# Delta-rule attention with a gated MLP on one core: one written list in place of a planner, and inverses widened two steps at a time

## The chip, the core and the metric

The kernel runs on one core of a Trainium2 chip. The metric is the device time of one execution in microseconds (us). The engines are named as the profile names them: PE (matmul; PEld is its weight load), DVE (VectorE), ACT (ScalarE), POOL (GpSimd) and SP, which issues the DMAs.

## What is computed

Thirty-two heads (batch 4, 8 heads, 48 columns each) run a delta rule over 768 positions; the result goes through an MLP whose gate mixes positions:

```
for t in range(S):
    y[:, :, t] = einsum('bhd,bhde->bhe', q[:, :, t], state)
    v_old = einsum('bhde,bhd->bhe', state, k_n[:, :, t])
    state = state + beta[:, :, t] * einsum('bhd,bhe->bhde', k_n[:, :, t], v[:, :, t] - v_old)
h = maximum(x @ w_in, 0)                 # x: y of all heads side by side, 4 x 768 x 384
u, v = h[..., :512], h[..., 512:]
v_s = einsum('ts,bsd->btd', w_spatial, layernorm(v)) + b_spatial
out = (u * v_s) @ w_out                  # 4 x 768 x 384
```

`k_n` is `k` divided by its norm. Weights `w_in` and `w_out` arrive as 64-bit floats and are decoded on the chip.

## The kernel before, in words

The 768 positions are cut into 12 chunks of 64. Inside a chunk the recurrence is solved by a 64x64 triangular inverse for each head, so that only the 48x48 state passes from one chunk to the next. Sixteen heads fill one pass over the tiles, so there are 24 *steps*: steps 0 to 11 are the 12 chunks of the first two batches, steps 12 to 23 those of the last two.

**Preparing.** The inverses are made for four steps at a time, in 6 *groups* (`prep`). For a group the PE forms the products of the keys (tile `ke` or `bn`, `kk`); ACT or DVE copy them from PSUM into a tile `xt`; a DVE transposition (L537) brings the 32x32 diagonal blocks into a layout, `la`, in which each of the 128 partitions holds whole blocks. A chain of small instructions (L545 to L555) works out the norms. Then the blocks are inverted column by column on all partitions at once, two DVE instructions a column (L574, L579; POOL does rows 16 to 31 beside it). Where `g < G16` (the first two groups) only 16x16 blocks are inverted this way (L587, L592), half the work, and a pair of PE blocks (`widen16`, 32 program matmuls each) makes 32x32 out of them. The DVE transposes back (L606). `widen` makes 64x64 out of 32x32: a DVE transposition into `tn` (L635), 16 matmuls of 32x32, a negation on ACT into `pi`, 16 more, and two copies.

**A step** (`step`): the PE forms k·state (`a`), DVE subtracts it from v (L738), the PE multiplies by the inverse (`b`), ACT evicts to `w` (L767), the PE forms the new part of the state (`c`), DVE adds it to `s` (L780), and only then can the next step's `a` run. `kqt` (L712 masks it) and `pu` make the output, which goes to `xs`. Each of these blocks is 16 program matmuls on two to four sub-tiles of the PE; an fp32 matmul leaves two records in the trace, so a block has 32.

**The MLP.** After every second step `mlp(J)` runs 128-row *dense* matmuls, 18 of 512 columns and 36 of 256; the gate of two batches (`mlp_g`, `mlp_o`) can start after step 11, that of the other two after step 23.

**Order.** All matmuls stand on line 486 (`mm`), all DMAs on line 381 (`ld`). `P.add` only records an instruction with a duration, a priority and its dependencies. `Plan.run` then lists them: it repeatedly takes, over all engines, the ready instruction that could start first by its own estimate, and among equals the one with the smaller priority, into which the table `TUNE` goes. An instruction with two possible engines (`both`: DVE or POOL) goes to the one that would end it sooner. Each engine executes its instructions in the order listed.

Of the kernel before, what the change touches and what calls it, by code (L numbers as in the profile page):

```python
# [25 lines left out]
NJ = NP // 2  # L26
KR = 112
EPS = 1e-6
G16 = 2
FILL = False  # L30

LOW, HIGH, KEEP, FORCE = 0.37, 0.74, 0.5, 0.4
WARM = 12.0
BIAS = 1.5

TUNE = [
# [10 lines left out]
]  # L47
GATE = 3.413
OTHER = {"DVE": "POOL", "POOL": "DVE"}
# [4 lines left out]

class Op:
    __slots__ = ("i", "eng", "dur", "fn", "pr", "deps", "out", "n", "acq", "rel", "give", "start", "end", "lag", "port", "kb", "took", "inst", "alt", "line", "bias", "act")


class Hold:
    def __init__(self):  # L60
        self.unit = None
        self.refs = 0
        self.t = 0.0
        self.tile = None
# [7 lines left out]
class Plan:  # L72


    LAT = {"PE": 0.2, "DVE": 0.06, "ACT": 0.08, "POOL": 0.08, "SP": 0.0, "X": 0.0}

    def __init__(self):
        self.ops, self.w, self.r, self.pools = [], {}, {}, {}
        self.filler, self.warm_from = None, 0.0
        self.kinds = {}  # L80

    def pool(self, name, units):
        self.pools[name] = [[0.0, u] for u in units]

    def add(self, eng, dur, fn, rd=(), wr=(), pr=0.0, acq=(), rel=(), give=(), lag=0.0, port=False, kb=0, inst=32, bias=0.0, act=1.0):
        o = Op()
        o.bias = bias
        o.kb, o.inst, o.act = kb, inst, act
        o.line = fn.__code__.co_firstlineno if fn is not None else 0
        o.alt = {}  # L90
        for e, d in dur.items() if isinstance(dur, dict) else ((eng, dur),):
            c = self.kinds.setdefault((e, o.line), len(self.kinds)) if fn is not None else -1
# [18 lines left out]
        for _, h in rel:  # L111
            h.refs += 1
# [962 lines left out]
```

## Time and profile before

| | |
|---|---|
| time, median of 3 runs | 526.24 us (526.05 to 527.23) |
| profiled execution | span 522.3 us |
| PE busy | 452.3 us, 87% of the span |
| DVE busy | 294.9 us, 56% |
| ACT busy | 246.8 us, 47% |
| POOL busy | 169.8 us, 32% |

The profiled execution is one execution; its span runs from the first to the last instruction, and the time of a run is 3.9 us more than this span. PE's granted clock changes between its two levels within the span; a block of small matmuls takes about 0.6 us at one and 1.0 us at the other.

### The profile page before, as it was taken

How to read it: one execution, taken by the hardware profiler on the slowest of the kernel's cores; microseconds unless marked ns; L12 is line 12 of the kernel's file. 1: busy time of each engine (PE TensorE's matmuls, PEld its weight loads, DVE VectorE, ACT ScalarE, POOL GpSimd, SP SyncE). 2: the span in 40 equal slices, each digit the busy share in tenths (PEclk: the TensorE clock that was granted, in tenths of full speed). 3: DMA queues.
4: the chain of work that ended last, by engine and by line, in shares of the span. 5: the costliest groups of instructions: out<-in, count | busy, mean ns of one | idle time of the engine just before them, and what ended most of it. 6: DMA issues, size and time to landing. Idle time of an engine off the chain costs nothing.

```text
span 522.3 us, 21286 instructions
## 1 busy us (share of the span) xinstructions
PE 452.3 (87%) x9544; PEld 410.4 (79%) x9544; DVE 294.9 (56%) x700; ACT 246.8 (47%) x530; POOL 169.8 (32%) x262
## 2 busy tenths in 40 slices
PE   4046789689889898877999899997999999999997
PEld 4045777679678787766989788886999899999997
DVE  3866675375775458876687777741353321453340
ACT  3947743653267735984235320842217874032111
POOL 2546765254416455465434642500000000000000
PEclk9999956655997879996899979996999999999999
DMA  8630254233241424104230422022000002001002
GB/s 291 236 124 26 90 198 131 64 107 110 75 128 35 156 102 141 52 2 151 75 120 33 152 90 95 31 75 82 11 1 0 2 1 75 16 1 62 31 0 92
DMA packets 16027, 42.63 MB, mean 82 GB/s; under 512 B 3392, under 2 KB 7616, under 8 KB 15936
## 3 DMA queue, kind: packets, MB, share of 16 engines
q1 hardware_dynamic: 15936, 41.27, 23.7%
q8 instruction: 75, 1.23, 1.0%
q14 instruction: 16, 0.13, 0.1%
HBM read 35.36 MB, written 4.72 MB: 77 GB/s over the span
## 4 chain that ended last, share of the span: by engine, by line
PE 77%; DVE 9%; issue 6%; ACT 3%; DMA 3%; SPq 1%; DVEq 0%; ACTq 0%
PE ps L486 77%; DMA vf<-in_w_in 2%; DVE prod L574 1%; SPq L381 1%; DVE ps L579 1%; DVE xt L606 1%; DVE ps L592 1%; DVE prod L587 1%; DMA ke<-in_k_t 1%; DVE pt L712 1%; ACT vr L866 0%; DVE nl L551 0%; ACT xs L797 0%; ACT ut L898 0%; ACT xt L513 0%
## 5 line engine op out<-in xcount | busy, mean ns | idle before, releaser
L486 PE MATMUL ps<-wsp_h,vf 128*128 128x256 f32 x480 | 99.4, 290 | 0.1
L486 PEld LDWEIGHTS ps<-wsp_h,vf 128*128 128x128 f32 x480 | 79.0, 191 | 2.0 <-issue 0.3
L486 PE MATMUL ps<-wsp_l,vf 128*128 128x256 f32 x240 | 68.1, 284 | 0.0
L486 PEld LDWEIGHTS ps<-wsp_l,vf 128*128 128x128 f32 x240 | 46.1, 192 | 0.1
L698 POOL TENSOR_TENSOR bn<-bn,nn 128x384 f32<-128x384 f32 x24 | 20.4, 852 | 74.6 <-DMA bn<-in_bun 36.9
L933 DVE TENSOR_TENSOR gt<-ps,bbc 128x512 f32<-128x512 f32 x24 | 16.6, 690 | 49.3 <-PE ps L486 49.1
L579 DVE TENSOR_TENSOR ps<-ps,prod 128x192 f32<-128x192 f32 (+13 forms) x120 | 39.5, 329 | 3.6
L574 DVE TENSOR_TENSOR prod<-ps,la 128x192 f32<-128x192 f32 (+13 forms) x120 | 38.4, 320 | 3.3
L486 PE MATMUL ps<-ke 48*64 48x64 f32 x704 | 19.1, 262 | 23.4 <-DVE pt L712 17.7
L486 PEld LDWEIGHTS ps<-ke 48*64 48x64 f32 x704 | 15.9, 168 | 27.5 <-DVE pt L712 17.9
L486 PE MATMUL ps<-bn 48*64 48x64 f32 x832 | 22.6, 259 | 7.4 <-DMA bn<-in_k_t 3.7
L767 ACT COPY w<-ps 128x384 f32<-128x384 f32 x24 | 11.5, 479 | 36.9 <-PE ps L486 36.9
L938 ACT CAST xt<-gt 128x512 fp32r<-128x512 f32 x12 | 7.5, 622 | 43.3 <-DVE gt L936 43.3
L780 DVE TENSOR_TENSOR s<-s,ps 112x384 f32<-112x384 f32 x20 | 11.0, 550 | 29.3 <-PE ps L486 29.3
L486 PE MATMUL ps<-tn,xt 32*32 32x32 f32 x768 | 21.2, 214 | 7.3 <-issue 3.3
L486 PE MATMUL ps<-wout_h,g 128*128 128x384 f32 x96 | 27.1, 355 | 0.0
L486 PEld LDWEIGHTS ps<-bn 48*64 48x64 f32 x832 | 19.1, 169 | 10.0 <-issue 7.5
L486 PEld LDWEIGHTS ps<-tn,xt 32*32 32x32 f32 x768 | 18.1, 128 | 10.2 <-DVE tn L635 3.9
L486 PE MATMUL ps<-wout_h,xt 128*128 128x384 f32 x96 | 25.5, 336 | 0.0
L656 ACT COPY xt<-ps 32x256 f32<-32x256 f32 x48 | 17.4, 362 | 16.2 <-PE ps L486 15.6
L797 ACT COPY xs<-ps 112x512 f32<-112x512 f32 x22 | 12.9, 586 | 23.3 <-PE ps L486 22.2
L486 PE MATMUL ps<-s,bn 48*64 48x48 f32 x704 | 19.0, 254 | 5.6 <-DVE s L780 4.7
(176 smaller groups left out, 1201.4 us busy)
## 6 DMA issues: line engine op xcount, KB each, us to landing
bn<-in_bun SPq DMA_DIRECT2D x22, 896.0 KB, 5.0
ke<-in_k_t SPq DMA_DIRECT2D x22, 256.0 KB, 3.0
out<-ob SPq DMA_DIRECT2D x24, 192.0 KB, 1.9
vf<-in_w_in SPq DMA_DIRECT2D x6, 512.0 KB, 10.3
g<-in_w_sp SPq DMA_DIRECT2D x3, 768.0 KB, 5.5
g<-in_w_out SPq DMA_DIRECT2D x4, 384.0 KB, 3.6
bn<-in_bun SPq DMA_DIRECT2D x2, 640.0 KB, 5.0
xs<-xs SPq DMA_DIRECT2D x66, 16.0 KB, 2.9
```

What stands on the lines that cost most here:

```text
L381: return P.add("SP", SPD, lambda: nc.sync.dma_start(out=out_() if callable(out_) else out_, in_=in_() if callable(in_) else in_), rd, wr, ...
L486: nc.tensor.matmul(o, l, r, start=start, stop=stop)
L574: P.add(eng, cost, lambda: e.tensor_tensor(out=dst if j == i0 else pt, in0=w[:, :n, j : j + 1].broadcast_to([128, n, m]), in1=la3[:, j, j ...
L579: P.add(eng, cost, lambda: e.tensor_tensor(out=dst, in0=dst, in1=pt, op=ALU.add), rd=[pk], wr=[key], pr=p0 + 2)
L587: P.add("DVE", cost, lambda: nc.vector.tensor_tensor(out=dst if j == 0 else pt, in0=w4[:, :, :n, j : j + 1].broadcast_to([128, 2, n, m]), ...
L656: P.add("ACT", 0.37, lambda r=r: nc.scalar.copy(out=x8_()[r, :, 32:64], in_=v3(pe[r, 0:256], 32)), rd=["pe0"], wr=[("fo", s, a)], pr=pr)
L698: P.add("", {"DVE": 0.56, "POOL": 0.84}, bias=BIAS, fn=lambda e: ENG[e].tensor_tensor(out=v, in0=v, in1=n.unsqueeze(2).broadcast_to([128, ...
L767: P.add("ACT", 0.48, lambda: nc.scalar.copy(out=v3(w, 192), in_=v3(pc, 512)[:, :, 0:192]), rd=["pc"], wr=[("w", s % 2)], pr=pr)
L780: P.add("DVE", 0.55, lambda: nc.vector.tensor_tensor(out=sv, in0=sv, in1=pv, op=ALU.add), rd=["pc"], wr=["S"], pr=pr)
L797: nc.scalar.copy(out=x.rearrange("p (s j t) -> p s j t", s=4, j=2)[0:KR, :, :, s % 2 * 64 : s % 2 * 64 + 64], in_=pq.rearrange("p (s c) -> ...
L933: P.add("DVE", 0.69, lambda: nc.vector.tensor_tensor(out=gt(), in0=v3(bank(h.unit), 256), in1=bbc[0][:, th * 256 : th * 256 + 256].unsquee ...
L938: P.add("ACT", 0.6, lambda: nc.scalar.copy(out=gv(gg)[0][:, hs], in_=gt_[t.unit]), rd=[kk], wr=[("gh", b, th, half)], pr=q)
```

## The change

1. **Order.** `Plan.run`, its estimates and `TUNE` are gone. A table `ORDER` of some 2,560 numbers lists every instruction of every engine; a number is four times the instruction's index plus the choice among its engines. `Plan.issue` walks through it. The table's rows tell a reader nothing; the fences below show what it does.
2. **Half-turned chunks.** On the host the odd chunks' keys, values and betas are rolled by 32 positions, and the mask of `kqt` differs by parity. So `widen` can be made for an even and an odd step at once: one goes from the lower 32 rows of a half to the upper 32, the other from the upper to the lower, and their matmuls alternate over four sub-tiles of the PE. One transposition of 128x512 takes the place of two of 128x256, and 32 program matmuls in one block that of two blocks of 16.
3. **16x16 blocks only in the first group** (`G16 = 1`). The second group's blocks are inverted as 32x32.
4. **Rows split 12/20** (`RS = 12`) in the inverses of the other five groups: DVE has rows 0 to 11, POOL rows 12 to 31 (16 and 16 before).
5. **Contractions of 64 rows** in place of 48 for keys and state; the added rows are zero.
6. The norm chain loses a copy; the scaling of `la` is two instructions of 128x512, each free to go to DVE or POOL; the first evictions are all on ACT. Of the instructions that may go to either engine the list gives DVE many more. Counted over the whole program: PE 5,674 program matmuls before and 5,418 now, DVE 702 and 740 instructions, ACT 484 and 489, POOL 267 and 303, DMAs 166 and 166. The 256 missing matmuls are those of `widen16`.

```diff
-G16 = 2
+G16 = 1
+RS = 12
...
+ORDER = """
+0 12 24 20 36 48 60 908 8 16 4 76 28 904 288 40 32 1124 52 548 44 340 64 56
...
+    def issue(self, order):
+
+        for o in self.ops:
+            for _, h in o.rel:
+                h.refs += 1
+        for i, sel in order:
+            o = self.ops[i]
+            for p, h in o.acq:
+                h.unit = self.pools[p].pop(0)
+            if o.fn is not None:
+                e = list(o.alt)[sel]
+                o.eng = e
+                o.fn(e) if len(o.alt) > 1 else o.fn()
...
+        for k in range(2):
+            P.add({"DVE": 0.69, "POOL": 1.3}, lambda e, k=k: ENG[e].tensor_mul(
+                out=la3[:, 16 * k : 16 * k + 16], in0=la3[:, 16 * k : 16 * k + 16], in1=dv.unsqueeze(1).broadcast_to([128, 16, 32])),
+                rd=["dv", "la"], wr=[("las", k)], due=p0)
...
             for j in range(31):
-                lanes("DVE", "wp", wp, prod, 0, j)
-                if j >= 16:
-                    lanes("POOL", "whi", w3[:, 16:32], prod2, 16, j)
...
+                lanes("DVE", "wp", wp, prod, 0, RS, j, p0 + 1 + 0.65 * j)
+                if j >= RS:
+                    lanes("POOL", "whi", w3[:, RS:32], prod2, RS, 32, j, p0 + 1 + 0.65 * j)
...
     def widen(s):
...
+        P.add({"DVE": 0.86}, lambda: nc.vector.transpose(out=tq, in_=v()[:, :, 0:4:3, :]), rd=[("x", (s + i) % (2 * GP), q) for i in range(2) for q in ("d0", "z1")], wr=["tn"], due=due)
+        WAY = ((near, far, 1), (far, near, 2))
 
         def e():
...
+            x = v()
             for q in range(NS):
                 for a in range(2):
-                    r, lo = slice(a * 64, a * 64 + 32), slice(a * 64 + 32, a * 64 + 64)
-                    mm(pe[lo, q * 32 : q * 32 + 32], x8[r, q, 32:64], tn[r, q * 32 : q * 32 + 32])
...
+                    for par, (i, o, f) in enumerate(WAY):
+                        mm(pe[o(a), q * 32 : q * 32 + 32], x[i(a), q, f, :], tq[i(a), q, par, :])
...
+        x[:, 1::2] = np.roll(x[:, 1::2], CH // 2, axis=6)
```

The order on the PE at the start, before. The `16x16` and `32x16` rows are the first group's `widen16` (`xt_153` the tile of its blocks, `bbc` the tile that holds a copy of them, `gi` the negated product), `ke` rows are the next group's key products, `32x32` rows are `widen`:

```order
L486 MATMUL ps<-xt_153,bbc 16x16 x32
L486 MATMUL ps<-ke 64x64 x16
L486 MATMUL ps<-xt_153,bbc 16x16 x32
L486 MATMUL ps<-gi,bbc 32x16 x32
L486 MATMUL ps<-ke 64x64 x16
L486 MATMUL ps<-xt_153,bbc 16x16 x32
L486 MATMUL ps<-gi,bbc 32x16 x32
L486 MATMUL ps<-tn,xt_153 32x32 x16
L486 MATMUL ps<-gi,bbc 32x16 x32
L486 MATMUL ps<-xt_153,bbc 16x16 x32
L486 MATMUL ps<-xt_153,pi 32x32 x16
```

The same place now (`ob_82` holds what `gi` held, `tn_71` is the transposition of two steps; `bn_74,xt_88` is the `b` of step 0):

```order
L437 MATMUL ps<-ke 64x64 x80
L437 MATMUL ps<-xt_88,bbc 16x16 x64
L437 MATMUL ps<-ob_82,bbc 32x16 x64
L437 MATMUL ps<-xt_88,bbc 16x16 x64
L437 MATMUL ps<-ob_82,bbc 32x16 x64
L437 MATMUL ps<-tn_71,xt_88 32x32 x32
L437 MATMUL ps<-xt_88,tn_71 32x32 x32
L437 MATMUL ps<-bn_74,xt_88 64x48 x16
```

The second group's key products have moved ahead of the first group's widening, `widen16` runs for two steps in a row, and one `widen` block has 32 program matmuls where it had 16.

The order on the DVE between step 0 and the inverse of the second group, before. `L780` is the state of step 1, `L738` the subtraction of step 2, `L712` a mask, `L555` the scaling of `la`, and with `L587` the second group's 16x16 inverse begins:

```order
L551 TENSOR_SCALAR nl<-t_94 128x32
L564 STREAM_TRANSPOSE nn_98<-nl 128x32
L552 TENSOR_TENSOR t_94<-nl 128x32
L553 RECIPROCAL t_94<-t_94 128x32
L780 TENSOR_TENSOR s<-s,ps 112x384
L554 TENSOR_TENSOR dv<-t_94,bl_91 128x32
L738 TENSOR_TENSOR bn_76<-bn_76,ps 128x384
L712 TENSOR_TENSOR pt_74<-ps,fl 128x512
L555 SCALAR_TENSOR_TENSOR la<-la,dv 128x1024
L587 TENSOR_TENSOR ps<-ps,la 128x2x15
L587 TENSOR_TENSOR prod<-ps,la 128x56
```

The same place now. `L369` are low parts of split weights, which POOL made before; `L609` is the transposition for steps 2 and 3, `L527` one half of the scaling, `L547` and `L552` the second group's 32x32 inverse, and `L769` the state of step 0:

```order
L369 TENSOR_TENSOR win_l<-ut_338,win_h 128x512
L667 MEMSET xt_88 32x8x32 x2
L369 TENSOR_TENSOR wsp_l<-g_232,wsp_h 128x768
L524 RECIPROCAL t_93<-t_93 128x32
L525 TENSOR_TENSOR dv<-t_93,bl_91 128x32
L609 STREAM_TRANSPOSE tn_71<-xt_88 128x512
L527 TENSOR_TENSOR la<-la,dv 128x512
L547 TENSOR_TENSOR ps<-ps,la 128x31
L547 TENSOR_TENSOR prod<-ps,la 128x60
L552 TENSOR_TENSOR ps<-ps,prod 128x2x30
L769 COPY s<-ps 112x384
```

The inverse of the second group now begins ahead of the state of step 0, where it stood behind the state of step 1, and the six `win_l` and the first `wsp_l` have come onto the DVE ahead of it.

## Rows read from the trace of the kernel before

**Rows 1.** The head of the page and the first line of its part 4 (the chain that ended last, shares of the span).

```profile
span 522.3 us, 21286 instructions
...
PE 77%; DVE 9%; issue 6%; ACT 3%; DMA 3%; SPq 1%; DVEq 0%; ACTq 0%
```

**Rows 2.** Busy time of each engine (x instructions) in two stretches, before and behind the point at which the inverses of the fourth group have been transposed back; columns: stretch, its length, PE, PEld, DVE, ACT, POOL, granted clock, DMA share, GB/s.

```profile
0.00:225.00 225.00, 169.31 (x4991) 145.72 (x4991) 148.81 (x372) 132.23 (x278) 111.71 (x164) 0.83 0.37 120
...
225.00:522.30 297.30, 283.00 (x4553) 264.69 (x4553) 146.13 (x329) 114.52 (x252) 58.04 (x99) 0.95 0.16 53
```

**Rows 3.** What the PE waited for in the second stretch (225 to 522.3 us): total us, times, longest.

```profile
PE ps L486 <- issue: 8.7, 9, 3.3
```

**Rows 4.** The last long piece of the chain in order of time: start, length, what.

```profile
357.94 160.84 PE ps L486 x1420
```

**Rows 5.** What the DVE waited for in the first stretch (0 to 225 us): total us, times, longest.

```profile
DVE xt L682 <- PE ps L486: 13.7, 6, 4.1
...
DVE tn L635 <- PE ps L486: 10.0, 7, 3.6
...
DVE s L780 <- PE ps L486: 7.9, 7, 2.3
...
DVE pt L712 <- PE ps L486: 6.2, 7, 2.5
...
DVE bn L738 <- PE ps L486: 3.9, 7, 1.2
```

**Rows 6.** Groups of DVE instructions by line over the whole span: line, engine, operation, out<-in, shapes, count | busy us, mean ns of one | idle us before them and what ended it. L574/L579 are the two instructions of a full column of the inverse, L587/L592 those of a 16x16 column.

```profile
L579 DVE TENSOR_TENSOR ps<-ps,prod 128x192 f32<-128x192 f32 (+13 forms) x120 | 39.5, 329 | 3.6
...
L574 DVE TENSOR_TENSOR prod<-ps,la 128x192 f32<-128x192 f32 (+13 forms) x120 | 38.4, 320 | 3.3
...
L592 DVE TENSOR_TENSOR ps<-ps,prod 128x56 f32<-128x56 f32 (+7 forms) x28 | 7.4, 264 | 0.9
...
L587 DVE TENSOR_TENSOR prod<-ps,la 128x56 f32<-128x56 f32 (+7 forms) x28 | 7.2, 256 | 0.9
...
L738 DVE TENSOR_TENSOR bn<-bn,ps 128x384 f32<-128x384 f32 x22 | 12.2, 554 | 14.1 <-PE ps L486 11.6 <-POOL prod L574 1.1 <-issue 0.8
...
L818 DVE TENSOR_TENSOR xl<-xs,xh 128x768 fp32r<-128x768 f32 x2 | 1.9, 954 | 1.5 <-ACT xh L817 1.5
...
L936 DVE TENSOR_TENSOR gt<-gt,ut 128x512 f32<-128x512 f32 x18 | 12.4, 692 | 0.6
...
L664 DVE STREAM_TRANSPOSE bbc<-xt 128x256 f32<-128x256 f32 x8 | 3.4, 426 | 0.0
...
L682 DVE TENSOR_TENSOR xt<-xt,ps 128x128 f32<-128x128 f32 x8 | 2.3, 287 | 14.2 <-PE ps L486 13.7 <-issue 0.4
...
L860 DVE TENSOR_SCALAR st<-st 128x2 f32<-128x2 f32 x12 | 2.0, 170 | 0.4
...
L537 DVE STREAM_TRANSPOSE la<-xt 128x1024 f32<-128x1024 f32 x6 | 11.9, 1988 | 5.4 <-ACT xt L364 4.0 <-POOL xt L364 1.3
...
L635 DVE STREAM_TRANSPOSE tn<-xt 128x256 f32<-128x256 f32 x24 | 10.7, 444 | 17.7 <-PE ps L486 15.5 <-POOL xt L616 1.9
...
L522 DVE MEMSET ps<- 128x256 f32 x1 | 0.3, 272 | 0.1
```

**Rows 7.** Two shapes of L574 kept apart (same columns).

```profile
L574 DVE TENSOR_TENSOR prod<-ps,la 128x240 f32<-128x240 f32 x8 | 3.3, 407 | 0.2
...
L574 DVE TENSOR_TENSOR prod<-ps,la 128x112 f32<-128x112 f32 x8 | 2.2, 271 | 0.2
```

**Rows 8.** POOL instructions by line, whole span (same columns).

```profile
L579 POOL TENSOR_TENSOR wl<-wl,prod 128x28 f32<-128x28 f32 (+7 forms) x56 | 15.7, 281 | 4.0
...
L411 POOL TENSOR_TENSOR wsp_l<-g,wsp_h 128x768 fp32r<-128x768 f32 x6 | 10.8, 1815 | 0.1
```

**Rows 9.** Three small DVE instructions of the norm chain, 32 to 232 us (same columns).

```profile
L552 DVE TENSOR_TENSOR t<-nl 128x32 f32<-128x32 f32 x4 | 3.1, 773 | 0.0
...
L551 DVE TENSOR_SCALAR nl<-t 128x32 f32<-128x32 f32 x4 | 3.1, 772 | 0.1
...
L550 DVE TENSOR_TENSOR t<-t,sq 128x32 f32<-128x32 f32 x4 | 2.5, 623 | 0.1
```

**Rows 10.** The same instruction L550 at two times in the DVE's timeline: start, us, engine, line.

```profile
60.86 1.20 DVE L550 TENSOR_TENSOR t<-t,sq 128x32 f32<-128x32 f32 x1
...
109.96 0.19 DVE L550 TENSOR_TENSOR t<-t,sq 128x32 f32<-128x32 f32 x1
```

**Rows 11.** The POOL's timeline at the first of these times.

```profile
60.73 1.27 POOL L411 TENSOR_TENSOR win_l<-ut,win_h 128x512 fp32r<-128x512 f32 x1
```

**Rows 12.** Blocks in the PE's timeline: start, us, engine, line, out<-in, shapes, count of records (a program matmul leaves two).

```profile
34.82 0.72 PE L486 MATMUL ps<-xt,bbc 32*16 32x16 f32 x64
...
51.99 1.06 PE L486 MATMUL ps<-tn,xt 32*32 32x32 f32 x32
...
339.59 0.69 PE L486 MATMUL ps<-xt,pi 32*32 32x32 f32 x32
...
396.37 0.86 PE L486 MATMUL ps<-win_h,la 128*128 128x512 f32 x3
...
397.06 0.86 PE L486 MATMUL ps<-win_l,la 128*128 128x512 f32 x3
```

**Rows 13.** A wait in the DVE's timeline between two columns of the inverse of the third group; brackets: idle before it and what ended it.

```profile
119.64 0.45 DVE L635 STREAM_TRANSPOSE tn<-xt 128x256 f32<-128x256 f32 x1 [2.87 <-PE ps L486]
```

More of the change, by code (lines that the diff above doesn't have):

```diff
@@ L52 @@
 NU = 6
+ORDER = """
[109 rows of a table added]
+"""
 class Op:
-    __slots__ = ("i", "eng", "dur", "fn", "pr", "deps", "out", "n", "acq", "rel", "give", "start", "end", "lag", "port", "kb", "took", "inst", "alt", "line", "bias", "act")
+    __slots__ = ("i", "alt", "sel", "fn", "deps", "acq", "rel", "give", "lag", "port", "kb", "kind", "n", "due", "line", "eng")
 class Hold:
@@ L290, in both, with small, due_of @@
     return {"DVE": dve_t(n), "POOL": pool_t(n)}
+def small(d=0.2):
+    return {"DVE": d, "POOL": d + 0.02}
+def due_of(s):
+    return 45.0 + (9.5 * s if s < 12 else 9.5 * 12 + 13.0 * (s - 12))
 @with_exitstack
@@ L413, in load_f64, with split_w @@
-    def load_f64(key, hi, lo, src, n, pr, spr, acq, raw, e, st):
+        nc.gpsimd.memset(masks, 1.0)
+        for par in range(2):
+            for k in range(4):
+                m = masks[k * 32 : k * 32 + 32, par * CH : par * CH + CH]
+                nc.gpsimd.affine_select(
+                    out=m, in_=m, pattern=[[1, CH]], compare_op=ALU.is_gt, fill=0.0, base=-32 * ((k + par) % 2), channel_multiplier=-1,
+                )
+    P.add({"POOL": 2.0}, mk_mask, wr=["mask"], due=28)
+    def split_w(src_, key, hi, lo, n, due, rel):
+        P.add({"ACT": act_t(n)}, lambda: nc.scalar.copy(out=hi, in_=src_()), rd=[key], wr=[(key, "h")], due=due)
+        P.add(both(n), lambda e: ENG[e].tensor_sub(out=lo, in0=src_(), in1=hi), rd=[key, (key, "h")], wr=[(key, "l")], due=due, rel=rel)
@@ new lines, in prep, with shift @@
+        diag = lambda: xg()[:, :, 0:4:3, :]
+        def shift(e, a, par, back):
+            rows, i, o = PARK[par]
+            i, o = (o, i) if back else (i, o)
+            copy(e, xg()[rows(a), :, o, :], xg()[rows(a), :, i, :])
+        for par in range(2):
+            for a in range(2):
+                P.add({"ACT": 0.6, "POOL": 0.6}, lambda e, a=a, par=par: shift(e, a, par, False), rd=xp("d1", par), wr=[("za", par, a)], due=dk + 13)
+        za = [("za", par, a) for par in range(2) for a in range(2)]
@@ L553, in prep @@
[L553 to L558 removed]
+        p0 = dk + 17
@@ L877, in mlp_u @@
-    def mlp_u(J, half, x, b0, pr):
+        kk = ("vr", i)
+        P.add({"ACT": 0.62}, lambda: nc.scalar.copy(out=full_(f)[:, 0:DH], in_=raw_(r)), rd=[kk] + ([("gdone", 0)] if i // NT == 1 else [("vh", 2 * NT + k) for k in range(NT)] if i // NT == 3 else []), wr=[("vh", i)], due=due, acq=[("full", f)])
+        P.add(both(512), lambda e: ENG[e].tensor_sub(out=full_(f)[:, DH : 2 * DH], in0=raw_(r), in1=full_(f)[:, 0:DH]), rd=[kk, ("vh", i)], wr=[("vl", i)], due=due + 1, rel=[("raw", r)])
+    def mlp_u(J, half, x, b0, due):
@@ L878, in mlp_u @@
         th, o = divmod(J % NT, 2)
         h = Hold()
-        if o == 0 and half == 0:
+        first = o == 0 and half == 0
+        if first:
             for j in range(2):
```

714 lines of the change are left out of this document (274 added, 440 removed), and 118 rows, old and new, of tables (ORDER, TUNE).

## The prediction

> **What bounds the kernel now.** I read the head of the page and the chain first: most of the 522.3 us run through the PE [rows 1]. That says where the end is set, not what each stage waits for, so next come the engines' busy times on both sides of 225 us, where the inverses of the fourth group have been transposed back [rows 2]. Behind it the PE works 283.0 of 297.3 us, and what it waits for is mainly "issue" [rows 3]; the last 160.8 us are one unbroken run of matmuls [rows 4]. That stretch costs what its matmuls cost. Ahead of it the PE is busy 169.3 of 225.0 us, the DVE 148.8 and the POOL 111.7. No engine is full: the inverse on the DVE, the widening on the PE and the step chain wait for each other in turn. The DVE's idle 76.2 us are mostly waits for the PE: before the sums of the 16x16 widening (L682), the transpositions for the 32x32 widening (L635), the state, the mask and the subtraction [rows 5]. The change works on the first stretch through the DVE and on the second through the PE, so I cut the sum there and ask which instructions the new order puts on which side.
>
> **The second stretch.** Counted in the two programs, the order puts almost the same PE work behind the fourth transposition: 17 more dense matmuls of 512 columns and 52 more key products, otherwise the same, and no 16x16 widening in either. A 512-column matmul costs (397.06 - 396.37) / 3 = 0.23 us [rows 12], 17 of them 3.9 us. The 52 products are 3.25 blocks of 32 records; at the 0.69 us of a small block [rows 12] that is 2.2 us. Against them, six pairs of steps are widened here: 24 blocks of 32 records become 12 of 64. The trace has no 32x32 block on four sub-tiles. The nearest row is the 16-column block of 64 records on four sub-tiles, 0.72 us; a block of 32 takes 0.69 us at the higher clock and 1.06 at the lower [rows 12]. So one pair of blocks saves 2 x 0.69 - 0.72 = 0.66 to 2 x 1.06 - 0.72 = 1.40 us, or nothing if the four sub-tiles take turns. Both clocks occur (0.95 granted on average [rows 2]); I take 1.0, so 12.0 us. The 64-row contractions change neither the count nor the columns of a block; I cost them at nothing, and if the rows of a block do count, its 0.69 us bounds the error. The issue waits (8.7 us) I leave as they are. Sum: 297.3 + 3.9 + 2.2 - 12.0 = 291.4 us.
>
> A rule speaks against this term. The 64-record block with 16 columns took no longer than 0.72 us although its four row groups wrote one PSUM bank [rows 12], so there the groups did not take turns. The Trainium skill (TensorEngine Tiling (Array Packing), Gotcha 1: PSUM Pressure) says that different row tiles cannot access the same PSUM bank simultaneously; the new block writes one bank from four row groups as well. By the rule the 12.0 us would be 0; the trace disagrees for 16 columns, and no run here shows 32. That outcome is the fourth rival.
>
> **The first stretch, DVE work.** Counted on the DVE up to the fourth transposition back, by kinds.
>
> Inverses: a full one costs (39.5 + 38.4) / 4 = 19.5 us, a 16x16 one (7.4 + 7.2) / 2 = 7.3 [rows 6]. The second group changes from one to the other, +12.2. With 12 rows in place of 16 a group has 1,300 elements fewer; the slope is (407 - 271) / 128 = 1.06 ns each [rows 7], so -1.4 for each of three groups, -4.2. Together +8.0 us. POOL's share of rows grows, but POOL was half idle [rows 2].
>
> Moved from POOL: 9 scalings of v (as L738, 0.554), 5 `xl` and 5 `wsp_l` (0.954), 6 `win_l`, 10 decoding steps and 3 low parts of v (0.692), 7 instructions of 128x384 (0.554) and 13 zero fills (0.27) [rows 6]: 5.0 + 9.5 + 13.1 + 3.9 + 3.5 = 35.0 us.
>
> Gone: four 16x16 widenings (0.426 + 0.287), 26 small instructions on `st` that POOL gets (0.17), two evictions (0.69), and one `la` transposition that now stands behind the mark (1.99) [rows 6]: 2.9 + 4.4 + 1.4 + 2.0 = 10.7 us. Six transpositions of 128x512 for twelve of 0.444 [rows 6] I cost at no difference (bounds: 6 x 0.44 us less or as much more). The copy that the norm chain loses stays uncounted, and the DMAs are the same 166 on the same queue.
>
> Relief: L552, L551 and L550 take 0.62 to 0.77 us on average in this stretch [rows 9]; the same L550 takes 1.20 us at 60.86 and 0.19 at 109.96 [rows 10], and at 60.86 a `win_l` runs on the POOL [rows 11]. The excess over 0.19 is (0.58 + 0.58 + 0.43) x 4 = 6.4 us; the bounds are no relief and all of it, and as the large POOL instructions leave, I take 5.
>
> DVE work: 148.8 + 8.0 + 35.0 - 10.7 - 5 = 176.1 us.
>
> **The first stretch, DVE idle.** Of 76.2 us, the wait for the 16x16 sums (13.7) halves with the number of groups: -6.9. The wait of L635 (10.0) halves with the number of transpositions: -5.0. The waits for state, mask and subtraction (7.9 + 6.2 + 3.9) depend on PE blocks; the PE loses 8 blocks of 0.72 us [rows 12] and 12.0 us of widening here, about a tenth of its 169.3, so -1.9. That leaves 62.4. The 35.0 us of moved work is not on the step chain and can be listed into these gaps, or not: the bounds are 0 and 35.0 us filled. The mean wait is 13.7 / 6 = 2.3 us at L682, 1.4 at L635, 1.1 at L780, 0.9 at L712, 0.6 at L738 [rows 5], and a moved instruction takes 0.27 to 0.95 us, so most gaps hold one. I take three quarters, 26.3. Idle 36.1, and the stretch is 176.1 + 36.1 = 212.2 us. The start is in this sum: the first group's columns are now interleaved with the decoding of weights, so step 0 comes later and the steps behind it sooner.
>
> The DVE executes in order: what the list puts behind an instruction that waits is held with it. The trace has it in the third group's inverse: between two of its column instructions L635 waited 2.87 us for the PE [rows 13]. In the changed order every wait that the list misjudges holds the columns, and with them the next group's steps.
>
> **Sum.** 212.2 + 291.4 = 503.6 against 522.3 us. The median of the runs is 526.24 - 522.3 = 3.9 us above the span, so 507.5 us.
>
> **Rivals.** First: *The moved work does not fit (slower).* The DVE becomes the bound of the first stretch: none of the 35.0 us is filled, 212.2 + 26.3 = 238.5, and 238.5 + 291.4 + 3.9 = 533.8 us. It decides from the point where the first stretch exceeds 522.3 - 291.4 = 230.9 us, that is, where under 8 of the 35.0 us fit. For it: in-order holding [rows 13], and a DVE that must be busy 176.1 of 230.9 us, 76%, where it was 66%. Against it: most waits named are for the PE, which has less to do here.
>
> Second: *It fits better than I take.* All orders stand in one list, so also the old work can move into gaps. If a fifth of the old idle stays, 15.2 us, and the 12 widenings save the 1.40 us of the lower clock: 176.1 + 15.2 + 286.6 + 3.9 = 481.8 us. For it: no wait of the first stretch but the start is unavoidable. Against it: every column of an inverse depends on the one before.
>
> Third: *The moved instructions wait for POOL.* The 45 moved ones that read two tiles in SBUF run beside POOL's columns, which are more now. If each is held for one POOL column, 0.281 us [rows 8], that is 12.6 us, and the relief of 5 does not come: 503.6 + 17.6 + 3.9 = 525.1 us. For it: L550 at 60.86 [rows 10]. Against it: the large POOL instructions (1.8 us, [rows 8]) are the ones that leave. The Trainium skill (SBUF — State Buffer, Who interferes with whom) says that a DVE instruction with two SBUF inputs and a GpSimd instruction that reads SBUF contend for one port, and that whoever comes first keeps it for its whole instruction. The trace agrees on L550, 0.19 against 1.20 us.
>
> Fourth: *The four sub-tiles take turns.* The 12.0 us are not saved, nor the 5.0 and 1.9 us of the waits: 503.6 + 18.9 + 3.9 = 526.4 us, no change. Against it: the 0.72 us block [rows 12].
>
> **Chances.** My forecast 0.44, the rivals in order 0.18, 0.24, 0.08, 0.06. Around my own number I allow half the moved work more or less, about 17 us either way (490 to 525). From 480 to 531 us holds 8 of 10: below lies the better half of rival 2, above the worse half of rival 1. A measurement of this kernel can tell about 0.2% from no change, 525.2 to 527.3 us. Faster: 0.43 + 0.24 + 0.05 + 0.03 = 0.75; within it 0.05; slower 0.18 + 0.02 = 0.20.
>
> **What would show it.** The fourth transposition back should end near 212 us and the rest take 291. A `widen` block of 64 records should take about 0.7 us; 1.3 shows rival 4. The DVE's busy time up to that point should be about 176 us and its idle 36; rival 1 shows as 60 us of idle in which column instructions stand behind waits for the PE, rival 3 as moved instructions well above 0.69 us while POOL runs. I am wrong altogether if the second stretch differs much from 291 us, since then the PE's efficiency has changed and not its work.

## The result and the profile after

The changed kernel takes 471.01 us (median of 5 runs, 468.66 to 471.53) against 526.24 of the kernel before: a ratio of 0.895, interval 0.892 to 0.898. The forecast was 507.5 us with a range of 480 to 531, so the time lies below the range. The direction was right; the gain is 55 us where 19 were forecast. The profile is of the fastest of the five executions (468.66 us). Ratios, here and below, leave out runs more than 1.5% above the fastest of their kernel; medians are over all runs.

The head of the page and the first line of its part 4, as in [rows 1]:

```profile
span 466.8 us, 20267 instructions
...
PE 405.2 (87%) x9032; PEld 366.1 (78%) x9032; DVE 306.4 (66%) x738; ACT 246.3 (53%) x535; POOL 125.9 (27%) x298
...
PE 68%; ACT 14%; DVE 12%; issue 4%; DMA 1%; DVEq 0%; ACTq 0%
```

The fourth transposition back now ends at 191.9 us in place of 225.2. Every stretch is cut 0.3 us ahead of that end; this cut is called the mark below. Busy times before and behind it, columns as in [rows 2]:

```profile
0.00:191.60 191.60, 136.78 (x4377) 116.01 (x4378) 160.91 (x417) 127.75 (x273) 74.95 (x182) 0.78 0.41 136
191.60:466.80 275.20, 268.42 (x4658) 250.13 (x4656) 145.53 (x322) 118.60 (x263) 50.98 (x116) 1.00 0.18 60
```

The first stretch is 33.4 us shorter than in [rows 2], the second 22.1 us. The forecast had 12.8 and 5.9. In the second the granted clock is 1.00 (the higher level, 2.4 GHz, all the way) where it was 0.95, and PE is busy 268.4 of 275.2 us. What the PE waited for there (total, times, longest), beside the 8.7 us of issue in [rows 3]:

```profile
PE ps L437 <- issue: 1.8, 3, 1.2
PE ps L437 <- DVE pt L701: 0.6, 1, 0.6
```

What the DVE waited for in the first stretch, to set against [rows 5]; `L767` is the state (before L780), `L701` the mask (L712), `L661` the sum of the 16x16 widening (L682):

```profile
DVE s L767 <- PE ps L437: 4.3, 3, 1.9
...
DVE pt L701 <- PE ps L437: 1.3, 3, 0.7
...
DVE xt L661 <- ACT win_h L368: 0.9, 1, 0.9
```

Groups of DVE instructions over the whole span, to set against [rows 6]; `L609` is the transposition for two steps, `L369` and `L388` came from POOL:

```profile
L552 DVE TENSOR_TENSOR ps<-ps,prod 128x60 f32<-128x60 f32 (+9 forms) x150 | 45.9, 306 | 3.8
...
L609 DVE STREAM_TRANSPOSE tn<-xt 128x512 f32<-128x512 f32 x12 | 8.4, 700 | 3.2 <-PE ps L437 2.5 <-POOL xt L591 0.5
...
L369 DVE TENSOR_TENSOR win_l<-ut,win_h 128x512 fp32r<-128x512 f32 x6 | 5.5, 930 | 0.0
...
L388 DVE TENSOR_TENSOR ut<-ut 128x512 f32<-128x512 f32 x5 | 3.3, 676 | 0.0
```

The three small instructions of the norm chain from 32 to 232 us, which took 623 to 773 ns in [rows 9]:

```profile
L523 DVE SCALAR_TENSOR_TENSOR t<-nl 128x32 f32<-128x32 f32 x4 | 0.8, 190 | 0.1
...
L521 DVE TENSOR_TENSOR t<-t,sq 128x32 f32<-128x32 f32 x4 | 0.8, 188 | 0.1
...
L522 DVE TENSOR_SCALAR nl<-t 128x32 f32<-128x32 f32 x4 | 0.7, 174 | 0.0
```

And two `widen` blocks of 64 records in the PE's timeline (start, us), one at each clock level; two blocks of 32 took 2 x 1.06 and 2 x 0.69 us [rows 12]:

```profile
54.17 1.08 PE L437 MATMUL ps<-xt,tn 32*32 32x32 f32 x64 [1.31 <-ACT tn L628]
...
61.62 0.75 PE L437 MATMUL ps<-xt,tn 32*32 32x32 f32 x64
```

### The profile page after: what moved, and what is told of

Same layout as the page of the kernel before. It is cut to its first block, busy times and chain, and to the rows that moved or that the text cites. A ratio compares the mean times of both kernels' runs of the same rounds, so it can differ in the third digit from the quotient of the medians.

```text
span 466.8 us, 20267 instructions
## 1 busy us (share of the span) xinstructions
PE 405.2 (87%) x9032; PEld 366.1 (78%) x9032; DVE 306.4 (66%) x738; ACT 246.3 (53%) x535; POOL 125.9 (27%) x298
## 4 chain that ended last, share of the span: by engine, by line
PE 68%; ACT 14%; DVE 12%; issue 4%; DMA 1%; DVEq 0%; ACTq 0%
PE ps L437 68%; ACT xt L325 4%; DVE ps L552 1%; DVE prod L547 1%; ACT xt L632 1%; ACT gt L838 1%; DVE xt L579 1%; DVE pt L701 1%; DVE win_l L369 1%; ACT ut L381 1%; ACT ut L379 1%; ACT ut L380 1%; DMA bn<-in_k_t 1%; DVE xt L591 1%; ACT xh L804 1%
## 5 line engine op out<-in xcount | busy, mean ns | idle before, releaser
L552 DVE TENSOR_TENSOR ps<-ps,prod 128x60 f32<-128x60 f32 (+9 forms) x150 | 45.9, 306 | 3.8
L915 DVE TENSOR_TENSOR gt<-ps,bbc 128x512 f32<-128x512 f32 x24 | 16.5, 688 | 47.1 <-PE ps L437 47.0
L547 DVE TENSOR_TENSOR prod<-ps,la 128x60 f32<-128x60 f32 (+9 forms) x150 | 44.6, 297 | 4.0
L552 POOL TENSOR_TENSOR wl<-wl,prod 128x36 f32<-128x36 f32 (+4 forms) x90 | 33.8, 375 | 6.4
L437 PE MATMUL ps<-ke 64*64 64x64 f32 x704 | 18.4, 255 | 19.0 <-ACT xt L325 10.4
L936 ACT COPY ob<-ps 128x384 f32<-128x384 f32 x24 | 11.5, 479 | 40.1 <-PE ps L437 36.0
L547 POOL TENSOR_TENSOR prod<-wl,la 128x36 f32<-128x36 f32 (+4 forms) x90 | 30.7, 342 | 7.0
L754 ACT COPY w<-ps 128x384 f32<-128x384 f32 x24 | 11.5, 477 | 36.0 <-PE ps L437 36.0
L437 PE MATMUL ps<-bn 64*64 64x64 f32 x832 | 20.9, 248 | 10.3 <-DMA bn<-in_k_t 3.7
L437 PEld LDWEIGHTS ps<-wout_h,g 128*128 128x128 f32 x128 | 23.2, 188 | 0.8
L325 ACT COPY xt<-xt 32x512 f32<-32x512 f32 (+1 forms) x35 | 20.0, 573 | 4.0 <-DVE xt L661 2.0
L437 PE MATMUL ps<-wout_l,g 128*128 128x384 f32 x64 | 21.9, 344 | 0.0
L437 PE MATMUL ps<-win_h,xh 128*128 128x512 f32 x60 | 21.8, 463 | 0.0
```

Source lines behind the costliest of these rows:

```text
L325: (nc.scalar.copy if e == "ACT" else ENG[e].tensor_copy)(out=out_, in_=in_)
L437: nc.tensor.matmul(o, l, r, start=start, stop=stop)
L547: P.add({eng: cost}, lambda: e.tensor_tensor(out=dst if j == i0 else pt, in0=w[:, :n, j : j + 1].broadcast_to([128, n, m]), in1=la3[:, j, ...
L552: P.add({eng: cost}, lambda: e.tensor_tensor(out=dst, in0=dst, in1=pt, op=ALU.add), rd=[pk], wr=[key], due=due)
L754: P.add({"ACT": 0.48}, lambda: nc.scalar.copy(out=v3(w, 192), in_=v3(pc, 512)[:, :, 0:192]), rd=["pc"], wr=[("w", s % 2)], due=due + 2)
L915: P.add({"DVE": 0.69}, lambda: nc.vector.tensor_tensor(out=gt(), in0=v3(bank(h.unit), 256), in1=bbc[0][:, th * 256 : th * 256 + 256].unsqu ...
```

## The experiments

In the diffs, "list" is the table `ORDER`; where an experiment relists instructions, the fence says in words what stands where.

**Do the four sub-tiles work side by side, and what is it worth?** In `e`, and likewise in `f_`, the even step's matmuls go first and the odd step's behind them:

```diff
-            for q in range(NS):
-                for a in range(2):
-                    for par, (i, o, f) in enumerate(WAY):
+            for par, (i, o, f) in enumerate(WAY):
+                for q in range(NS):
+                    for a in range(2):
```

> The changed kernel, but a widening block does all 32 records of the even step first and then the 32 of the odd step, so that two sub-tiles alternate in place of four. Same instructions, same order of all else. If the four sub-tiles run side by side (block of 64 records 0.75 us at the higher clock), a block becomes 1.3 us and 24 blocks add 7 us in the second stretch, where the PE is full, and up to 7 more in the first: 478 to 485 us. If they take turns anyway: 471 us, within 1.5.

Measured: 475.71 us, ratio 0.907 (0.901 to 0.913), mark at 195.9, second stretch 277.9 us. The block at the higher level:

```profile
200.72 1.11 PE L437 MATMUL ps<-tn,xt 32*32 32x32 f32 x64 [0.44 <-DVE tn L609]
```

1.11 in place of 0.75 us, so interleaved matmuls of four sub-tiles do run side by side. The whole is worth 4.7 us, less than expected. Of that, 2.7 us lie behind the mark; the rest lies ahead of it, where even an unchanged list differs by as much between runs (see the next experiment). Rival 4 falls, but the pairing is a small part of the 55.

**Does the moved work matter?** The 28 decoding and splitting instructions of lines 369, 387 and 388 that the list gives DVE go to POOL, at the same places:

```diff
-(list) L369, L387, L388: DVE
+(list) L369, L387, L388: POOL
```

> The changed kernel with 28 instructions of the weights' decoding and splitting (win_l, wsp_l, wout_l and the two last decoding steps) listed at the same places, but on POOL, where the kernel before had them; the DVE loses some 21 us of work ahead of the fourth transposition back. Theory 'DVE-bound': the first stretch shortens by 10 to 20 us, 451 to 461 us. Rival 'POOL in the way': with POOL busy the small DVE instructions take 0.6 to 0.8 us again in place of 0.19 and the later users wait for POOL, so nothing is gained or it is slower, 471 to 485 us.

Measured: 474.9 us, ratio 0.906 (0.899 to 0.914). The first stretch, columns as above:

```profile
0.00:196.40 196.40, 135.23 (x4376) 114.71 (x4377) 149.41 (x389) 127.53 (x273) 108.91 (x210) 0.78 0.40 133
```

DVE is 11.5 us less busy, and the mark comes 4.8 us later. How much of the 4.8 us is real is unsure: with the list untouched up to the mark it lay anywhere from 191.6 us (the changed kernel itself) to 196.6 (e5, e11 to e14 below). The run also brings waits of its own. From 49.2 us the PE waits 9.3 us for a negation on ACT (L628), which stands in ACT's list behind casts of weights (L368), and these wait 9.7 us in total for POOL's decoding (L388). So less work on DVE did not shorten the first stretch here; what it would bring without the waits for POOL is not shown.

**Rows of the inverse.** `RS = 12` back to 16:

```diff
-RS = 12
+RS = 16
```

> The changed kernel with RS = 16: DVE has rows 0 to 15 of the 32x32 inverses and POOL 16 to 31, the list otherwise as it is (POOL's lane instructions of columns 12 to 15 dropped). Forecast: 4.2 us less DVE work from 12 rows; here the five inverses get 1300 elements longer each at 1.06 ns, so DVE busy +4.1 us in the first three and the fourth transposition back 192 to 196. Theory 'DVE work decides the first stretch': 473-476 us. Rival 'POOL's columns end last': the split 12/20 leaves POOL 19 columns of up to 20 rows, and with 16 POOL ends sooner, so 467-471 us.

Measured: 471.54 us, ratio 0.897 (0.893 to 0.902). DVE is 4.9 us busier ahead of the mark (165.8) and the mark at 193.6; the mark fits the first expectation and the time lies nearer the second; by the time no difference can be told. 5 us more of DVE work do not show in it; POOL was 13.5 us less busy at once, and the run does not separate the two.

**Contractions of 64 rows**, back to 48 (a third place, in `qs`, likewise):

```diff
-        return t[d * 64 : d * 64 + 64, off + s * 64 : off + s * 64 + 64]
+        return t[d * 64 : d * 64 + 48, off + s * 64 : off + s * 64 + 64]
...
-                            st_[d * 64 : d * 64 + 64, q * 48 : q * 48 + 48])
+                            st_[d * 64 : d * 64 + 48, q * 48 : q * 48 + 48])
```

> The changed kernel with contractions of 48 rows in place of 64 for keys and state, list unchanged. Forecast: the rows of a block cost nothing, 469-473 us, second stretch 274-277. Rival 'rows count' (48-row operands cost the PE less or more): over 3 us of difference either way, and a pitch of small records off 17.1 ns.

Measured: 470.99 us, ratio 0.891 (0.885 to 0.897). No difference, as costed.

**One part alone in the kernel before:** `G16 = 1`.

```diff
-G16 = 2
+G16 = 1
```

> The kernel before with G16 = 1 and nothing else (its planner lists the rest; second group's blocks inverted as 32x32 on DVE and POOL, four widenings less). By the forecast's own prices: DVE +12.2 - 2.9 us and four waits of L682 less (some 7 us), so 0 to 5 us either way, 521-531 us. Rival 'the 16x16 pass was what held the second group': the second transposition back earlier than 87 us and 510-520 us.

Measured: 543.4 us, ratio 1.028 (1.020 to 1.036), above both expectations. The second transposition back ends at 105.6 in place of 87.7 us, the fourth at 242.2 in place of 225.2. The prices of the instructions don't give 17 us. That the planner's priorities, set for the other instructions, no longer fit is my reading; no run shows it.

**The changed instructions in the planner's order.** First try: before's greedy rule on the changed instructions, with the due times that the changed source carries as priorities.

```diff
-(list) as in the changed kernel
+(list) by before's Plan.run, priority = due
```

> The changed kernel's instructions in an order that the rule of the planner before lists (earliest start by its own estimates; among equals the earlier due time), with the engines of the free instructions chosen by it too; the list is written into the kernel as a table. Theory 'order': most of the gain is the order, so 500 to 515 us, with 60 us or more of DVE idle in the first stretch and stretches at the lower clock in the second. Rival 'instructions': the gain is in the widening and in the missing 16x16 blocks, so 470 to 485 us.

Measured: 529.93 us, ratio 1.010 (0.999 to 1.021), above both expectations, with a second stretch of 323 us. The due times are not the old planner's priorities, so this is not a fair copy of it. For a fairer one, priorities and tuned numbers of before were carried over instruction by instruction.

```diff
-(list) as in the changed kernel
+(list) by before's Plan.run, with before's priorities and TUNE
```

> All changed instructions, the whole order by before's planner with its tuned numbers carried over (in e4 the priorities were the due times). Theory 'order': the sum of e5 and e6, 495-525 us. Theory 'instructions': under 480 us.

Measured: 524.86 us (two runs, 520.29 and 529.43), beside 526.07 for the kernel before: theory "order". All changed instructions together, listed by the old planner with its old numbers, gain nothing that two runs can tell. The two stretches:

```profile
0.00:222.80 222.80, 144.11 (x4484) 121.64 (x4485) 131.31 (x347) 129.47 (x274) 138.28 (x248) 0.87 0.35 119
222.80:518.60 295.80, 271.02 (x4550) 253.77 (x4549) 89.81 (x223) 118.54 (x262) 154.24 (x218) 0.97 0.16 54
```

**Which stretch?** The changed list up to the mark, the planner's behind it:

```diff
 (list) as in the changed kernel up to the fourth transposition back
-(list) the rest as in the changed kernel
+(list) the rest by before's Plan.run, with before's priorities and TUNE
```

> The changed kernel's own list up to the fourth transposition back; everything behind it is listed by before's planner with its own priorities and tuned numbers, carried over instruction by instruction to the changed instructions (DVE or POOL chosen by the planner too). Theory 'order': the 16 us that the second stretch won beyond the forecast were won by the list, because it leaves the PE neither waits nor a stretch at the lower clock; so the first stretch stays near 192 us, the second rises from 275 to 287-300, PE waits in it rise from 2 to 8 us or more and some of it falls to the lower clock: 483-496 us. Theory 'instructions': paired widening and the other changed instructions make the PE run through whatever lists them; second stretch 273-280, 469-476 us.

Measured: 490.25 us, ratio 0.932 (0.926 to 0.938). The second stretch and the PE's largest wait in it:

```profile
193.30:489.40 296.10, 276.19 (x4632) 257.27 (x4628) 88.75 (x221) 119.41 (x263) 151.61 (x217) 0.97 0.17 56
```
```profile
PE ps L437 <- issue: 11.8, 9, 3.9
```

296.1 us, where the changed list makes 275.2 of the same instructions: 21 us by the list. The planner also chose the engines here: it puts 111 instructions on another one of DVE and POOL, and POOL is busy 151.6 us behind the mark, where it was 51.0. No run separates order and choice of engine in this stretch. What the PE waited for speaks for the order: 11.8 us are issue, and all waits for POOL and DVE together are 2.7 us. Now the reverse.

```diff
-(list) as in the changed kernel up to the fourth transposition back
+(list) the same instructions by before's Plan.run, with before's priorities and TUNE
 (list) the rest as in the changed kernel
```

> The reverse: what the changed list has up to the fourth transposition back is listed by before's planner with its carried-over numbers, and behind it stands the changed kernel's own list. Theory 'order': the planner's first stretch leaves the idle that the list has closed; fourth transposition back at 205-225 in place of 191.6, second stretch 270-277, 480-500 us. Theory 'instructions': 190-196 and 275, 470-476 us.

Measured: 518.69 us (513.28 to 522.25, and the profile is of the longest), ratio 0.984 (0.975 to 0.992), more than the theory asked for. The fifth transposition back, which the changed list places in both, ends at 309.3 in place of 257.7 us. So the relisted part lasts 51.6 us longer, until about 243 us, and some 277 us remain behind it, against 275.2 in the changed kernel. Not all of the 51.6 us belong to the order of the first part. Against the changed kernel e5 loses 19.2 us and e6 47.7, together 66.9, but e7, with the planner on both sides, loses 53.9, and its mark comes 31.2 us later. So the planner's order costs some 31 us ahead of the mark, and the rest of e6's loss seems to arise where the two lists meet. The planner put large instructions on POOL, so a second kernel gave each instruction the engine that the changed list gives it, and let the planner set the order alone.

```diff
 (engines) as in the changed kernel
-(list) as in the changed kernel up to the fourth transposition back
+(list) the same instructions by before's Plan.run, with before's priorities and TUNE
```

> As e6 (first stretch listed by before's planner, second by the changed list), but every instruction on the engine that the changed list gives it; the planner only sets the order. Theory 'choice of engine': e6 lost because its planner put large work on POOL (DVE busy 131 us, POOL 136 up to the mark, against 161 and 75); with the changed choice the fourth transposition back comes at 192-202 and the whole at 471-482 us. Theory 'order': the choice was not what cost, the waits between the engines are; the mark at 210-230, 490-520 us.

Measured: 519.78 us, ratio 0.982 (0.976 to 0.989): the choice of engine was not what cost. What the PE waited for up to 243 us, first of e6, then of e9:

```profile
PE ps L437 <- issue: 22.5, 16, 5.1
PE ps L437 <- DVE tn L609: 16.3, 1, 16.3
PE ps L437 <- ACT vr L828: 15.1, 1, 15.1
PE ps L437 <- DVE xt L579: 9.6, 1, 9.6
```
```profile
PE ps L437 <- DVE tn L609: 23.5, 2, 21.3
PE ps L437 <- DVE xt L579: 22.5, 1, 22.5
PE ps L437 <- issue: 16.1, 11, 2.7
```

Read the third number. Up to 243 us the PE of e6 idles 243 - 142.9 = 100 us, where the changed list has 54.8 up to its mark; three single waits of 9.6 to 16.3 us make 41 of these. The 15.1 us begin at 225.7 us, where the planner's part of the list ends. The other two stand in e7 as well, up to its mark:

```profile
PE ps L437 <- DVE tn L609: 16.3, 1, 16.3
PE ps L437 <- DVE xt L579: 8.3, 1, 8.3
```

The changed list's longest single wait up to its mark is 6.8 us. The PE's timeline of e6 around the 16.3 us, in brackets the idle before:

```profile
108.14 0.52 PE L437 MATMUL ps<-xl,win_h 128*128 128x256 f32 x3
124.92 1.07 PE L437 MATMUL ps<-tn,xt 32*32 32x32 f32 x64 [16.26 <-DVE tn L609]
```

From 95.1 to 108.7 us the planner lets the PE do one dense matmul after the other, and then nothing is left while the second group's inverse ends. In e9 the first such wait, 22.5 us, comes from the DVE: between two columns of the first inverse stand decoding steps of the weights,

```profile
42.29 0.24 DVE L565 TENSOR_TENSOR ps<-ps,prod 128x78 f32<-128x78 f32 x1
...
43.90 0.68 DVE L387 TENSOR_TENSOR ut<-ut,vf 128x512 f32<-128x512 f32 x1
44.62 2.17 DVE L388 TENSOR_TENSOR ut<-ut 128x512 f32<-128x512 f32 x1
...
48.64 0.21 DVE L560 TENSOR_TENSOR prod<-ps,la 128x56 f32<-128x56 f32 x1
```

and its transposition back ends at 53.2 in place of 33.0 us. Same work, same engines; what runs ahead of what decides. In e6 and e7 the second group is the first to come late by much: its transposition back ends at 121.0 and 119.6 us in place of 91.2.

**What in the second stretch?** 87 dense entries go behind the small blocks that follow them:

```diff
-(list) dense and small blocks in turn, mostly two small blocks in a row
+(list) each dense entry behind up to 8 small blocks that followed it
```

> The changed kernel with 87 of its dense PE entries of the second stretch moved behind the small blocks that follow them, as far as their readers allow, so that up to 8 small blocks (256 records) stand in a row where it was mostly 2; the same work and all else in the same order. Theory 'interleaving': long runs of small records bring the PE's issue waits back (1.8 us now, 8.7 in before, 11.8 in e5) and with them the lower clock; second stretch 280-292 us, 475-488 in all. Rival 'the small blocks' place among dense ones does not matter as long as something is ready': 274-277, 469-473 us. Between them, if the moved dense work is what covered a wait for DVE or ACT: the waits named show it.

Measured: 488.08 us, ratio 0.923 (0.916 to 0.930); second stretch 292.1 us, at the upper ends expected. The waits in it, and among them issue:

```profile
PE ps L437 <- ACT w L754: 3.7, 6, 0.6
PE ps L437 <- DVE pt L701: 3.6, 5, 1.9
PE ps L437 <- ACT xt L632: 3.5, 2, 1.9
...
PE ps L437 <- issue: 0.5, 2, 0.3
```

The size fits theory "interleaving", its mechanism doesn't: issue waits fell. What came back are many short waits for ACT and DVE between the blocks of a step, which the dense entries had covered. All waits of the PE there sum to 20.2 us, where the changed list has 3.0; the stretch is 16.9 us longer.

**Wait or clock?** Both changed together so far. One wait of known length on the step chain: the mask of step 16 is written again 6 or 12 times ahead of the subtraction.

```diff
+            for _ in range(6 if s == 16 else 0):
+                P.add({"DVE": 0.69}, lambda: nc.vector.tensor_tensor(out=pv, in0=qv.rearrange("p d (c t) -> p d c t", t=64), in1=mask.unsqueeze(1).unsqueeze(1).broadcast_to([128, 2, 4, 64]), op=ALU.mult), rd=[("kq", s), "mask"], wr=[("pt", s % 2)], due=due_of(s) + 1)
```

> The changed kernel with the mask instruction of step 16 (L701, 0.68 us) put on DVE 6 times more, writing the same again, just ahead of the subtraction of that step: about 3.6 to 4.1 us of delay on the step chain in the middle of the second stretch, all else as it is. Theory 'a wait costs itself': the PE stalls up to 4 us, part of it covered by the dense work listed there: span +0 to +4 us, granted clock of the second stretch stays 1.00. Theory 'a wait also costs the clock': a stretch at the lower level follows and the span rises by the delay and 2 to 6 us more.

> The same with 12 repeats, 7 to 8 us of delay. 'Costs itself': the second half of the delay has no cover left, so 3.6 to 4 us more than e13 and the clock still 1.00. 'Also the clock': a stretch at the lower level of several us, and over 6 us more than e13 unless e13 has it already; then what the lower level costs is read from the matmuls in that stretch.

Measured: 479.36 us (ratio 0.907, 0.901 to 0.914) and 481.91 us (0.913, 0.906 to 0.919). The part behind the mark and the PE's wait, first with 6, then with 12 repeats:

```profile
196.60:479.40 282.80, 270.57 (x4658) 252.12 (x4656) 149.93 (x328) 118.85 (x263) 50.64 (x116) 0.99 0.18 58
```
```profile
PE ps L438 <- DVE pt L704: 4.9, 1, 4.9
```
```profile
194.80:480.30 285.50, 269.57 (x4658) 251.32 (x4656) 153.72 (x334) 118.62 (x263) 50.64 (x116) 0.98 0.17 58
```
```profile
PE ps L438 <- DVE pt L704: 9.3, 1, 9.3
```

Against 275.2 us that is 7.6 and 10.3 us, for waits of 4.9 and 9.3. The clock does fall: behind the wait of the first run, three dense matmuls at 255.18 take 0.84 us where the same three take 0.52 later in this run:

```profile
255.18 0.84 PE L438 MATMUL ps<-xh,win_l 128*128 128x256 f32 x3
...
293.93 0.52 PE L438 MATMUL ps<-xh,win_l 128*128 128x256 f32 x3
```

The lower level lasts to 257.8 us. Going by the starts of the matmuls, one block of small ones and five such groups lose 1.9 us there in all; behind the longer wait the same work loses 1.5 us. By the stretches the loss beyond the wait is 2.7 and 1.0 us, but second stretches with an unchanged list differ by about 2 us between runs (275.2 in the changed kernel, 276.9 in e3). So "also the clock" is right for the shorter wait, at its lower end, and the longer wait costs the clock no more. A wait costs itself and one to three microseconds.

**A miss:** the filler matmuls that the kernel before can put into the PE's gaps, to see whether the clock alone helps.

```diff
-FILL = False
+FILL = True
```

> The kernel before, whose planner now also lists filler matmuls (their results are not used) into the PE's gaps. In the trace of before the second stretch has 30.8 us at the lower clock (237.8 to 251.4, 299.2 to 306.1, 357.3 to 367.5), in that of the changed kernel it has none. Theory 'clock': keeping the PE busy among the small blocks is worth some 10 to 15 us there, so 508 to 518 us, with a granted clock near 1.00 behind the fourth transposition back. Rival 'instructions': the clock is a side effect and the PE only had less to do; then the filler changes nothing or stands in the way, 524 to 535 us.

Measured: 536.98 us, ratio 1.024 (1.011 to 1.036), above both expectations. PE was 29 us busier but the granted clock no higher (0.94 in the second stretch), so this says nothing about the clock.

## Why the prediction was wrong

By the spans the forecast was 36.8 us too long: 20.6 us in the first stretch (212.2 for 191.6) and 16.2 in the second (291.4 for 275.2).

**The step that failed in the second stretch** is "the issue waits (8.7 us) I leave as they are", and with it the clock of 0.95 that the second stretch silently kept. I took the second stretch to cost what its matmuls cost. Going from each matmul's start to the next in the records, and counting what exceeds a matmul's usual step as waiting, the waits there fall from 9.4 to 2.0 us, and matmuls spend 28.2 us at the lower level before, none now. Worked out from the steps at either level (small records 18.1 and 29.2 ns, dense ones half as long at the higher): waits -7.4, the clock -9.6 outside the widening, small records -2.4 (2,368 at 17.1 in place of 18.1 ns), widening -9.2. The sum is -28.6; measured are -22.1, so 6.5 us were added. My 6.1 us of more work look like these, but the count behind them was wrong. The traces have 8 more dense matmuls of 512 columns behind the mark, not 17, 4 fewer of 256, and 48 more key products, not 52: some 3.4 us at the forecast's prices. The other 3 us are longer steps of the dense matmuls at the higher level (183 ns for 177 at 384 columns, 249 for 240 at 512). e5 shows that the gain is the list's: the same instructions take 296.1 us when the planner lists them. e12 shows one way: dense entries between the small blocks cover the waits of the step chain. e13 and e14 show that a single wait draws the lower level behind it, for 1.9 and 1.5 us; over the whole stretch before, the lower level cost more than the waits themselves.

**The widening (-12.0)** was close: 9.2. At the higher clock a pair saves 2 x 0.69 - 0.75 = 0.63 us; I took 1.0, because both levels occurred, and now only the higher does. The Trainium skill (TensorEngine Tiling (Array Packing), Gotcha 1: PSUM Pressure) has row tiles kept from one bank at the same time; the 0.75 us, and 1.11 when the two steps' matmuls stand apart (e2), disagree for this block.

**The step that failed in the first stretch** is to take it as the DVE's work plus its gaps, and the work as a sum of durations.

**DVE work (176.1 us)** was 160.9. I added 27.3 us of durations to a busy time of 148.8. The durations of the stretch rose from 156.2 to 177.6 us, by 21.4, which is 5.9 less than I added. "Relief" is in this: I took 5 us, but the small instructions of the norm chain became 5.2 us shorter (0.17 to 0.19 us where 0.62 to 0.77 stood [rows 9]), those of the decoding 2.9 us, and the copy that I left uncounted took 2.7. Other terms were off too; the moved work took 38.7 us for 35.0. The other 9.3 us are overlap: 16.7 us of the 177.6 lie on top of one another, where it was 7.4 of 156.2, and a busy time counts these once. The DVE's timeline shows it, here behind the mark: a column that needs the one before starts after its end, an instruction of other work starts before it:

```profile
280.47 0.22 DVE L547 TENSOR_TENSOR prod<-ps,la 128x60 f32<-128x60 f32 x1
280.73 0.23 DVE L552 TENSOR_TENSOR ps<-ps,prod 128x60 f32<-128x60 f32 x1
...
281.27 0.26 DVE L552 TENSOR_TENSOR ps<-ps,prod 128x87 f32<-128x87 f32 x1
281.44 0.68 DVE L915 TENSOR_TENSOR gt<-ps,bbc 128x512 f32<-128x512 f32 x1
282.03 0.26 DVE L547 TENSOR_TENSOR prod<-ps,la 128x112 f32<-128x112 f32 x1
282.21 0.54 DVE L767 TENSOR_TENSOR s<-s,ps 112x384 f32<-112x384 f32 x1
```

The first pair starts 0.04 us after the end, L915 0.09 us before it and L767 0.08. Of the 216 pairs of neighbouring column instructions L547 and L552 in the whole span none overlaps. I started from a busy time, which has the overlap taken out, and added durations, which don't.

**DVE idle (36.1 us)** was 30.7. Three quarters of the moved work filled into gaps was right in kind: the wait of the 16x16 sums went from 13.7 to 1.4 us, that of the transpositions for `widen` from 10.0 to under 1. But the working treated the first stretch as one engine's work plus its gaps. e3 takes 11.5 us of DVE work away and e8 adds 4.9, and neither moves the end that way beyond what runs differ by, though both change POOL's work too. What the order is worth there shows on the PE: in e7 the PE idles 78.7 us ahead of its mark, where the changed list has 54.8; two single waits make 24.6 of these, and issue waits 19.1 (6.3 in the changed list). This is read from the waits; no run fills them one by one. "The DVE executes in order" was in the prediction, as a danger; that the list would mend it on the PE was not costed.

**The rivals.** The second, "it fits better", named the side but not the mechanism; its 481.8 us lacked the second stretch. Its first stretch, 176.1 + 15.2 = 191.3 us, meets the measured 191.6 by luck: the work was 160.9 and the idle time 30.7. The first (moved work does not fit) and the fourth (sub-tiles take turns) fell. The third (moved instructions held by POOL) has the direction wrong: `ut` takes 0.676 us, as costed, and the small instructions became faster as POOL's large ones left. It is right for a few instructions: `win_l` takes 0.930 us where I costed 0.692, because one of six takes 2.29 us (at 42.87 us) beside a `wsp_l` of 2.15 us on POOL, and the others 0.62 to 0.69. The sentence that the forecast is wrong altogether if the second stretch leaves 291 us was the right test: "the PE's efficiency has changed and not its work".

**What stays open.** How far the planner's priorities, retuned for the changed instructions, could have come; how order and choice of engine share the 21 us of the second stretch; and the 5 us by which the first stretch of one and the same list differs between runs. What an issue wait ends with, the traces do show. Part 3 of the profile's page counts 75 transfers on the instruction queue q8 before and 71 now, each of 16 KB and one for 127 matmul records. In the 16 traces 208 of the PE's 209 issue waits over 0.3 us end 2.1 to 2.9 us after such a transfer starts, and no two of these transfers start less than 3.2 us apart. An estimate from these numbers: 127 small records at 17.1 ns take 2.2 us, so many small blocks in a row use instructions up faster than they come. Each of the three stretches at the lower level behind the mark before (from 238.1, 299.5 and 357.6 us) begins during such a wait or at most 1.1 us behind its end. No run changed the loading by itself.

## What to carry to other kernels

When a change replaces the order, don't forecast it from one engine's busy time and gaps: on every in-order engine look for the instruction at the head that waits longest, and ask what ready work stands behind it. Dense work that is free to move is worth most between the links of a dependent chain, where it covers the links' latency and keeps the PE at its higher clock. And test new instructions and a new order apart: here one part alone (`G16`) lost and all parts together gained nothing, in an order made for other instructions.

## What was not expected of the hardware

Neighbouring DVE instructions that don't depend on one another overlap by about 0.08 us, so other work listed between dependent columns costs that much less at its ends (16.7 us over the first stretch). One wait of 4.9 us on the PE was followed by a stretch at the lower clock level up to 257.8 us, some 4.5 us behind its end. And the PE's issue waits end with the loading of its instructions (2.1 to 2.9 us after a transfer starts). A run of small matmuls does not always bring them on: with up to 256 small records in a row in e12, between which the PE waited for ACT and DVE, these waits were 0.5 us behind the mark, while e5 had 11.8 us there and e6 22.5 up to 243 us.
